# A four-layer decode step and its gradients on one core: where the outer products of the gradients are begun, when the key and value rows are turned, and which queue carries rows of gradients

## The chip, the core and the metric

The kernel runs on one core of a Trainium2 chip. A core has a matrix engine (PE, which also has its own track for weight loads, PEld), a vector engine (DVE), a scalar engine (ACT), GpSimd (POOL) and a sync engine (SP). Each engine takes its instructions strictly in the order in which the program lists them, so an instruction that waits holds up everything behind it on that engine. DMAs are started by SP, ACT or POOL and are then carried out by 16 DMA engines. The metric is the time of one execution on the device in microseconds (us).

## The reference, cut to what matters

One token of width 1024 passes through attention A, MLP B, attention A and MLP B again, with the same weights both times, and then the gradients of all eight inputs are formed for a given output gradient.

```
x = x + A(layernorm(x));  x = x + B(layernorm(x))        # layer 0 of A, layer 0 of B
x = x + A(layernorm(x));  x = x + B(layernorm(x))        # layer 1 of A, layer 1 of B
out, vjp = jax.vjp(f, A_x, A_k_cache, A_v_cache, A_wq, A_wo, B_w1, B_b1, B_w2)
return out, *vjp(grad_out)
```

A has 32 query heads on 4 key-value heads of width 128 and looks at the last 4096 of 32768 cached positions. B is 1024 to 3584 to 1024 with the Mish activation. Everything is bfloat16. The outputs are large: `out_2` and `out_3` (gradients of the key and value caches, 33.5 MB each, zero except for the last 4096 positions of each head), `out_4` and `out_5` (gradients of wq and wo, 8.4 MB each), `out_6` and `out_8` (gradients of w1 and w2, 7.3 MB each), and three vectors. Since there is one token and there are two layers of each kind, the gradient of a weight is a sum of two outer products: a matrix product with only two rows to sum over.

## The kernel before

**Loads.** Weights come in chunks of 1 MB into `ring`, eight slots in SBUF. `Ring.want` queues loads, and `release` (line 77) frees a slot and starts the next queued load on SP's queue (line 68). In the last part of the kernel these are the seven chunks of w2 for the MLP backward of layer 0 (keys "2", 1), the eight chunks of wo for the attention backward of layer 0 (here: wo 0 to wo 7, keys "o", 3), and five chunks of wq (keys "q", 3, t from 0 to 4). Three more wq chunks were kept in the ring, already transposed, from the attention backward of layer 1.

**Zeros.** The zero parts of `out_2` and `out_3` are 56 stores of 1 MB from one zeroed tile. `zeros(n, after)` (line 240) starts n of them on POOL's queue, behind a tiny POOL copy that waits for the value `after`.

**Backward.** A chunk is multiplied by a vector either by DVE (`rowdot`, line 399, one block of 128 x 1024 against a broadcast vector) or by PE: `turned` (line 425) transposes eight 128 x 128 blocks into one of three PSUM buffers `BIG`, copies them back (`evac`, line 278, by DVE or ACT, whichever a running count of planned load says is less busy), and later multiplies them (`mv`, line 439).

The order of the part that the change touches is, in program order:

1. `attn_bwd(1, ...)`, the attention backward of layer 1, whose last loop calls `dn3(t)`.
2. The MLP backward of layer 0: seven chunks of w2, then `dn_b0` (line 810), which multiplies by w1 in SBUF (`W1`) and ends with the backward of the layer norm, `ln_bwd` (line 372). At t = 2 and t = 4 of its loop it starts to collect rows.
3. `attn_bwd(0, ...)`, the attention backward of layer 0: eight chunks of wo ("do"), the products with the values and the probabilities ("dp", hook `dp1`), the products with the keys ("dq", hook `dq1`), eight chunks of wq ("dn", hook `dn1`), and `ln_bwd` again.
4. The tail: `work(10000)` (line 1141) makes everything of the outer products that is left, with PSUM now divided into four `wide` buffers of 128 x 1024.

**Rows of gradients.** The outer products need their vectors as rows. The rows lie in `ROWS`, which is the SBUF of `W1` once w1 has been used; at bases 0, 32, 64 and 96 there are two partitions each (one for each layer). `rowize` (line 953) transposes a vector on PE, copies it to SBUF on ACT (line 959) and starts two small SBUF-to-SBUF DMAs (line 961); `take_back` (line 733) starts one DMA from a small DRAM buffer; `rowize_f` (line 781) does eight small transposes, one ACT copy (line 788) and two DMAs (line 790). All of these DMAs are on ACT's queue. In order there are: GB (2 DMAs), AC, NB, OC, NA (1 each), the two of `rowize_f`, GA (2, in the first step of "do") and DQC (2, in `dq1`).

**DMA lanes.** The DMAs of SP and ACT share eight semaphores in turn. A DMA therefore waits, in its queue, until the eighth DMA before it has landed. By the program's list of waits, and the turn in which the eight are given out, NB waits for wo 0 to have landed, OC for wo 1, NA for wo 2, and the two of `rowize_f` for wo 3 and wo 4.

**Units.** A unit is a product of 128 x 512 (or, with a `wide` buffer, 128 x 1024) of a gradient: one matmul for every 512 columns (line 993 for the four weight gradients; line 1042, two matmuls of 256, for the key and value caches) and one `evac` into a 1 MB staging slot. `store` sends a slot to HBM on SP's queue when it is full (line 971); four of the slots are sent in halves (line 976), once PSUM has been divided anew. No slot is full before the tail, so all stores of units are in the tail. `todo` holds four queues of such generators, and `work(n)` (line 1053) takes n units, going round the four queues. There are 304 units of 512 columns in all. `units_rows(96, ...)` makes `out_8` and reads rows GB and AC; `units_cols(64, ...)` makes `out_6` and reads rows NB and those of `rowize_f`; `units_rows(32, ...)` makes `out_5` from GA and OC; `units_cols(0, ...)` makes `out_4` from NA and DQC. `units_kv` needs the rows of probabilities and of vectors that `kv_rows` (line 1023) turns: 18 transposes and four evacuations for the values, and as many for the keys.

The units before the tail stand in three places: five in `units_b0` (line 802), which `ln_bwd` calls beside the norm of `dn_b0`; five in `dp1`; six in `dq1`.

## Time and profile before

| | us |
|---|---|
| three timed runs | 470.84, 472.27, 469.64; median 470.84 |
| the profiled execution | 475.21 |
| its span between first and last instruction | 473.4 |

| busy in the span | PE | PEld | DVE | ACT | POOL |
|---|---|---|---|---|---|
| us | 352.9 | 276.8 | 263.8 | 229.8 | 38.5 |
| share | 75% | 58% | 56% | 49% | 8% |

The DMA engines moved 183.51 MB in the span, a mean of 388 GB/s; in full stretches the rate is 410 to 425 GB/s. The profiled execution is 4.4 us above the median of the timed runs, so a difference is worked out inside the profile and then taken off the median.

How to read the views: a window line gives, for a stretch of time, the busy us of each engine with the number of instructions in brackets, then the clock that PE was granted (1.00 is full speed), the mean busy share of the 16 DMA engines, and the GB/s that they moved. A timeline line gives start, duration, engine, line of the kernel, operation, destination and source, and in square brackets how long the engine had been idle before it and what released it. `ACTq` and `SPq` are the instruction queues of ACT and SP, where DMAs are started. The chain of waits follows the work that ended last, backwards.

### The profile page before, as it was taken

The page shows a single profiled execution, that of the slowest core. Times are in us where ns is not written, and L with a number is a line of the kernel's source. Part 1 is how long each engine was busy: PE and PEld are TensorE (multiplying, and loading weights), DVE is VectorE, ACT ScalarE, POOL GpSimd, SP SyncE. Part 2 cuts the span into 40 slices and gives each one's busy share as a digit, 9 for nine tenths or more (in the row PEclk, how much of TensorE's full clock was granted, in tenths as well). Part 3 has the DMA queues.
Part 4 walks back from the last instruction along what each step waited for, and adds up shares of the span by engine and source line. Part 5 has one row for each costly group of instructions (what it writes and reads, how often), then busy time and mean ns, then how long its engine had stood idle before and what let it go on. Part 6 is the DMA issues. An engine that isn't in the chain of part 4 may idle for free.

```text
span 473.4 us, 14280 instructions
## 1 busy us (share of the span) xinstructions
PE 352.9 (75%) x6385; PEld 276.8 (58%) x6385; DVE 263.8 (56%) x522; ACT 229.8 (49%) x263; POOL 38.5 (8%) x85
## 2 busy tenths in 40 slices
PE   3746345696688896998797896497897769888880
PEld 3736334596687885898797896387677111111330
DVE  7405820462331259576275876074458678887880
ACT  2402001072146297484176461274154779788880
POOL 4000000000132030101100101002102000000000
PEclk9955555555555588797588555598558555555555
DMA  8999999999999999999999899559998999999997
GB/s 337 422 422 417 419 418 418 422 393 363 395 425 424 419 415 422 414 382 401 424 343 389 309 391 360 225 171 384 424 422 347 412 404 414 420 409 405 412 410 303
DMA packets 28219, 183.51 MB, mean 388 GB/s; under 512 B 3682, under 2 KB 3710, under 8 KB 9342
## 3 DMA queue, kind: packets, MB, share of 16 engines
q1 hardware_dynamic: 19654, 123.78, 65.3%
q0 software_dynamic: 8064, 58.72, 29.9%
q8 instruction: 50, 0.82, 0.7%
q10 hardware_dynamic: 440, 0.10, 0.1%
q14 instruction: 11, 0.09, 0.0%
HBM read 83.94 MB, written 98.62 MB: 386 GB/s over the span
## 4 chain that ended last, share of the span: by engine, by line
PE 50%; DMA 19%; DVE 15%; ACT 6%; issue 5%; ACTq 2%; SPq 0%; DVEq 0%
PE BIG L429 13%; DMA ring<-in_A_wo_dram 8%; PE wide L993 7%; PE BIG L580 4%; PE TP L441 4%; DMA VS<-in_A_v_cache_dram 4%; DVE junk L406 4%; DVE ring L284 4%; DMA W<-in_B_w_dram 4%; PE wide L1042 3%; PE MV L651 3%; ACT ring L287 2%; PE MV L599 2%; DVE VS L284 2%; PE MV L551 2%
## 5 line engine op out<-in xcount | busy, mean ns | idle before, releaser
L287 ACT COPY ring<-BIG 128x1024 bf16<-128x1024 bf16 x73 | 72.2, 1014 | 35.7 <-PE BIG L429 34.1
L429 PE MATMUL BIG<-ident_bf,ring 128*128 128x128 bf16 x872 | 80.8, 254 | 1.9 <-ACT W L287 1.1
L993 PE MATMUL wide<-W 2*128 2x512 bf16 x227 | 68.2, 607 | 11.6 <-ACT W L287 3.0
L429 PEld LDWEIGHTS <-ring 128*128 128x128 bf16 x952 | 70.8, 115 | 4.2 <-issue 3.2
L993 PEld LDWEIGHTS <-W 2*128 2x128 bf16 x240 | 11.8, 101 | 65.3 <-issue 64.6
L406 DVE CUSTOM_DVE_ANT_0 junk<-ring,SC 128x1024 bf16<-128x1024 bf16 x38 | 46.2, 1215 | 2.5 <-PE SC L311 1.1
L441 PEld LDWEIGHTS <-ring 128*128 128x128 bf16 x1024 | 38.5, 100 | 8.4 <-ACT ring L287 4.9
L284 DVE COPY ring<-BIG 128x1024 bf16<-128x1024 bf16 x36 | 24.8, 691 | 31.4 <-PE BIG L429 14.6
L284 DVE CAST ring<-wide 128x1024 bf16<-128x1024 f32 (+1 forms) x29 | 33.2, 1167 | 9.1 <-PE wide L993 5.8
L287 ACT CAST ring<-wide 128x1024 bf16<-128x1024 f32 (+1 forms) x35 | 33.7, 1003 | 7.1 <-PE wide L993 6.0
L287 ACT COPY KT<-BIG 128x1024 bf16<-128x1024 bf16 x22 | 21.6, 1015 | 30.9 <-PE BIG L580 29.3
L287 ACT COPY W<-BIG 128x1024 bf16<-128x1024 bf16 (+1 forms) x24 | 21.4, 1074 | 26.1 <-PE BIG L764 15.8
L248 POOL DMA_DIRECT2D out_dram<-zt x56 | 29.7, 536 | 11.3 <-DMA out_dram<-zt 10.6
L1042 PE MATMUL wide<-W 32*128 32x256 bf16 x122 | 25.7, 403 | 2.5 <-DVE ring L284 1.8
L551 PE MATMUL MV<-OC,ring 128*128 128x1 bf16 x512 | 16.5, 166 | 13.9 <-DMA ring<-in_A_wo_dram 12.8
L551 PEld LDWEIGHTS <-ring 128*128 128x128 bf16 x512 | 15.9, 106 | 14.6 <-DMA ring<-in_A_wo_dram 13.4
L1042 PEld LDWEIGHTS <-W 32*128 32x128 bf16 x128 | 13.4, 121 | 18.2 <-issue 14.4
L471 PE MATMUL MV<-NA,ring 128*128 128x1 bf16 x512 | 15.1, 165 | 10.7 <-DMA ring<-in_A_wq_dram 10.7
L599 PE MATMUL MV<-NB,W 128*128 128x1 bf16 x448 | 16.2, 172 | 9.3 <-DMA W<-in_B_w_dram 6.5
L406 DVE CUSTOM_DVE_ANT_0 junk<-ring,DSX 128x1024 bf16<-128x1024 bf16 x18 | 22.0, 1224 | 0.6
L599 PEld LDWEIGHTS <-W 128*128 128x128 bf16 x448 | 15.9, 118 | 9.8 <-DMA W<-in_B_w_dram 7.2
L471 PEld LDWEIGHTS <-ring 128*128 128x128 bf16 x512 | 14.3, 103 | 11.3 <-DMA ring<-in_A_wq_dram 11.3
(256 smaller groups left out, 552.3 us busy)
## 6 DMA issues: line engine op xcount, KB each, us to landing
out_dram<-zt POOLq DMA_DIRECT2D x56, 1024.0 KB, 14.3
ring<-in_A_wq_dram SPq DMA_DIRECT2D x27, 1024.0 KB
ring<-in_A_wo_dram SPq DMA_DIRECT2D x24, 1024.0 KB
ring<-in_B_w_dram SPq DMA_DIRECT2D x14, 1024.0 KB
W<-in_B_w_dram SPq DMA_DIRECT2D x8, 896.0 KB
out_dram<-ring SPq DMA_DIRECT2D x7, 1024.0 KB
out_dram<-ring SPq DMA_DIRECT2D x12, 512.0 KB
ring<-in_A_k_cache_dram SPq DMA_DIRECT2D x4, 1024.0 KB
```

The costliest lines, as they stand in the source:

```text
L248: nc.gpsimd.dma_start(dst, zt[:])
L284: nc.vector.tensor_copy(dst, src)
L287: nc.scalar.copy(dst, src)
L406: nc.vector.tensor_tensor_reduce(out=out, in0=a, in1=vec, scale=1.0, scalar=acc if i else 0.0, op0=ALU.mult, op1=ALU.add, accum_out=acc)
L429: nc.tensor.transpose(b[:, i * P:(i + 1) * P], block(w, i) if block else w[:, i * P:(i + 1) * P], ident_bf[:])
L441: nc.tensor.matmul(out, lhsT=w[:, i * P:(i + 1) * P], rhs=rhs_of(i), start=fresh[0], stop=last and i == n - 1, skip_group_check=True)
L471: nc.tensor.matmul(q_ps[:, h:h + 1], lhsT=ch[:, h * P:(h + 1) * P], rhs=NA[:, t, l:l + 1], start=(t == 0 and h == 0), stop=(t == TD - 1), ...
L551: nc.tensor.matmul(y_ps[:, dd:dd + 1], lhsT=ch[:, tt, dd * P:(dd + 1) * P], rhs=OC[:, h, l:l + 1], start=(h == 0 and dd == 0), stop=(h == ...
L580: nc.tensor.transpose(b[:, i * P:(i + 1) * P], T[:, g, 8 * b8 + i, :], ident_bf[:])
L599: nc.tensor.matmul(h_ps[:, fb:fb + 1], lhsT=f_block(W1[:, t], fb), rhs=NB[:, t, l:l + 1], start=(t == 0 and fb == 0), stop=(t == TD - 1), ...
L993: nc.tensor.matmul(b[:, 512 * i:512 * i + 512], lhsT=ROWS[base:base + 2, lo:lo + P], rhs=ROWS[base:base + 2, ro + 512 * i:ro + 512 * i + 5 ...
L1042: nc.tensor.matmul(b[:, k * 256:(k + 1) * 256], lhsT=RT[32 * g:32 * g + 32, a, tp, :], rhs=YS[32 * g:32 * g + 32, :], start=True, stop=Tru ...
```

## The change

- `dn_b0` calls `ln_bwd` without work beside its norm. `units_b0` is gone; its two generators (`out_8`, `out_6`) are put into the queues later, ahead of `attn_bwd(0, ...)`.
- `dp1` makes four units in place of five, and no longer calls `kv_rows` nor queues the units of the value cache. `dq1` makes no units, and no longer calls `kv_rows` nor queues those of the key cache.
- `ln_bwd` calls `beside` twice, once before and once after its matmul of the sums. Only `attn_bwd(0, ...)` hands one in: `units_a0`, four units each time. It adds 10 to DVE's planned load, so all eight go to ACT.
- The tail makes 20 units, turns the rows for the value cache and queues its units, makes 20 more, does the same for the key cache, and then makes the rest.
- The twelve DMAs of rows are started by SP in place of ACT, at the same points of the program.
- In `dn3`, one store of zeros waits for t = 5 in place of t = 3.

```
     ln_bwd:
+        if beside is not None:
+            beside()
         nc.tensor.matmul(TP[:, 128:130], lhsT=onesD[:], rhs=st[:], start=True, stop=True)
         if beside is not None:
             beside()
     take_back, rowize_f, rowize:
-        nc.scalar.dma_start(ROWS[...], ...)
+        nc.sync.dma_start(ROWS[...], ...)
-    def units_b0():
-        todo[3].append(units_rows(96, TF, out_8))
-        todo[2].append(units_cols(64, 7, out_6))
-        even()
-        load["D"] += 5
-        work(5)
     dn_b0:
-        return ln_bwd(dnp, sB0["n32"], sB0["rstd"], g, "B0", units_b0)
+        return ln_bwd(dnp, sB0["n32"], sB0["rstd"], g, "B0")
     dn3:
-        if t == 3:
+        if t == 5:
             zeros(1, dnp[:, t:t + 1])
     before attn_bwd(0, ...):
+    todo[3].append(units_rows(96, TF, out_8))
+    todo[2].append(units_cols(64, 7, out_6))
     dp1:
         zeros(4)
         stage_free.extendleft(VS[:, g].rearrange("p t d -> p (t d)") for g in range(G))
-        kv_rows(0, PX, DOC, DOST)
-        for g in range(G):
-            todo[g].append(units_kv(0, g, DOST, out_3))
-        work(5)
+        work(4)
     dq1:
         rowize(DQC, HQ, 0, NOFF)
         zeros(4, DQC[:, 0, 0:1])
-        kv_rows(1, DSX, QC, QST)
-        for g in range(G):
-            todo[g].append(units_kv(1, g, QST, out_2))
-        work(6)
+    def units_a0():
+        even()
+        load["D"] += 10
+        work(4)
     the tail:
     even()
+    work(20)
+    kv_rows(0, PX, DOC, DOST)
+    for g in range(G):
+        todo[g].append(units_kv(0, g, DOST, out_3))
+    work(20)
+    kv_rows(1, DSX, QC, QST)
+    for g in range(G):
+        todo[g].append(units_kv(1, g, QST, out_2))
     work(10000)
```

More of the change, by code (lines that the diff above doesn't have):

```diff
@@ L734, in take_back @@
         r = DR[name][:].rearrange("(n l) p -> l n p", l=2)
-        nc.scalar.dma_start(ROWS[base:base + 2, off:off + r.shape[1] * P].rearrange("l (n p) -> l n p", p=P), r)
+        nc.sync.dma_start(ROWS[base:base + 2, off:off + r.shape[1] * P].rearrange("l (n p) -> l n p", p=P), r)
     x3, st3, sA1 = attn_fwd(1, x2, st2, False, wo_hook1, last_da)
@@ L789, in rowize_f @@
         for l in range(2):
-            nc.scalar.dma_start(ROWS[64 + l:65 + l, NOFF:NOFF + F].rearrange("o (c j) -> o c j", j=512),
-                                rf[:, 512 * l:512 * l + 512])
+            nc.sync.dma_start(ROWS[64 + l:65 + l, NOFF:NOFF + F].rearrange("o (c j) -> o c j", j=512),
+                              rf[:, 512 * l:512 * l + 512])
     def store_f(col):
@@ L823, in dn_b0, with attn_bwd @@
                 rowize_f()
-        return ln_bwd(dnp, sB0["n32"], sB0["rstd"], g, "B0", units_b0)
+        return ln_bwd(dnp, sB0["n32"], sB0["rstd"], g, "B0")
     DENSE = 2
-    def attn_bwd(l, sv, g, wo_key, wq_key, wq_keep, hooks):
+    def attn_bwd(l, sv, g, wo_key, wq_key, wq_keep, hooks, beside=None):
         name = f"A{l}"
@@ L910, in attn_bwd @@
         bigs.remove(SC[1])
-        return ln_bwd(dnp, sv["n32"], sv["rstd"], g, name)
+        return ln_bwd(dnp, sv["n32"], sv["rstd"], g, name, beside)
     turned_q = set()
@@ L960, in rowize @@
         for l in range(2):
-            nc.scalar.dma_start(ROWS[base + l:base + l + 1, off:off + n * P].rearrange("o (t p) -> o t p", p=P),
-                                rt[l:2 * n:2, k, :])
+            nc.sync.dma_start(ROWS[base + l:base + l + 1, off:off + n * P].rearrange("o (t p) -> o t p", p=P),
+                              rt[l:2 * n:2, k, :])
     def store(dst, s, old, new, of, last):
@@ L1128, in dn1 @@
             todo[0].append(units_cols(0, 8, out_4))
-    g0 = attn_bwd(0, sA0, g1, ("o", 3), ("q", 3), (), dict(do=do1, dp=dp1, dq=dq1, dn=dn1))
+    def units_a0():
+        even()
+        load["D"] += 10
+        work(4)
+    g0 = attn_bwd(0, sA0, g1, ("o", 3), ("q", 3), (), dict(do=do1, dp=dp1, dq=dq1, dn=dn1), units_a0)
     g0b = sb([P, TD], BF16, "g0b")
```

## The prediction

> **What bounds the kernel now.** I read the DMA windows first, then the chain of waits in order of time, then the timeline around the place that both point to. Columns of the windows are explained above; these are of the kernel before.

> ```profile
> 270.00:280.00 10.00, 10.00 (x210) 10.00 (x209) 9.56 (x15) 6.19 (x7) 0.00 (x0) 0.50 1.02 386
> ...
> 290.00:300.00 10.00, 3.72 (x89) 3.32 (x86) 4.17 (x20) 1.00 (x1) 1.24 (x3) 0.50 1.01 410
> 300.00:310.00 10.00, 7.25 (x58) 5.30 (x59) 1.91 (x3) 4.71 (x8) 0.00 (x0) 0.58 0.24 98
> 310.00:320.00 10.00, 9.41 (x241) 9.34 (x239) 8.16 (x14) 7.71 (x8) 0.15 (x1) 1.00 0.65 212
> ...
> 370.00:460.00 90.00, 76.74 (x342) 19.57 (x341) 73.25 (x66) 77.22 (x83) 0.00 (x0) 0.50 1.01 412
> 460.00:470.00 10.00, 0.00 (x0) 0.00 (x0) 1.20 (x2) 0.73 (x1) 0.00 (x0) 0.50 1.01 407
> ```

> The DMA engines are full nearly throughout, and in the tail from 370 to 470 without a break, at 407 to 412 GB/s. The last arithmetic is over at about 461, and the DMAs still run 9 us. So the end is set by bytes: it moves by as much as DMA idle time is removed. The one large hole is from 302 to 316. The chain shows what lies in it:

> ```profile
> 289.12 0.76 ACTq L961
> 292.14 2.10 ACTq L735
> 294.28 1.01 ACT W L788
> 295.31 0.75 ACTq L790
> 296.10 5.90 DMA W<-W
> 303.38 1.07 PE BIG L993 x2
> 304.45 0.97 PE SC L311 x8
> ```

> and the timeline what is held up by it:

> ```profile
> 295.47 0.17 DVE L830 CAST GA<-g_B 128x8 bf16<-128x8 f32 x1
> 295.49 1.06 POOL L248 DMA_DIRECT2D out_dram<-zt  x2
> 302.10 0.25 PEld L993 LDWEIGHTS <-W 2*128 2x128 bf16 x4 [7.99 <-issue]
> 302.13 1.01 PE L993 MATMUL BIG<-W 2*128 2x512 bf16 x3 [7.93 <-DMA W<-W]
> ...
> 304.38 1.04 PE L311 MATMUL SC<-ident_bf,GA 128*128 128x128 bf16 x8
> ...
> 312.61 4.41 SPq L68 DMA_DIRECT2D ring<-in_A_wo_dram  x3
> ```

> The five units of `units_b0` need the rows of `rowize_f`. Those rows leave late, because ACT is busy issuing six small DMAs from 289.12 to 294.24 and only then makes its copy (line 788), and the second of their DMAs takes 5.90 us to land. PE stands for 7.93 us with the attention backward of layer 0 behind it, whose input GA is ready at 295.64. Meanwhile the ring is full: five wo chunks and three kept wq chunks. The next load (wo 5) starts only when wo 0 is released, at 312.61, 8.23 us after that attention's first matmul at 304.38. From 302 to 314 the DMA engines have nothing left.

> **The change part by part.**

> *No units at that norm.* The broadcast of GA then follows its cast as in the same code one stage earlier, where the cast at 262.32 is followed by PE at 262.56, 0.24 us later: 295.47 + 0.24 = 295.71 in place of 304.38. Gain 8.67 us on the path. wo 5 follows 8.23 us later, at 303.94. What is late next: the zeros of 295.49 (2 MB) keep the DMAs full until 302 as now, so a hole of about 2 us remains ahead of wo 5, and the slow start from 312.6 to 316 (shares 0.50 and 0.71 in two windows of 2 us) remains too.

> *dp1.* Now the products with DSX start at 338.11, behind 18 transposes and five units; the products with the values end at 333.35. With four units, PE needs three free `BIG` buffers and a fourth that ACT frees at about 334.6 (one ACT evacuation 0.59), so about 335.3. Gain 2.8 us. *dq1.* Now the broadcast ends at 343.02 and the wq transposes start at 348.52; with one small transpose (0.32) between, about 343.4. Gain 5.1 us.

> *Eight units beside the last norm.* PE stands for 1.94 us ahead of line 385 while DVE ends its row products, and the first four units fit there (matmuls of 0.25 to 0.45 us, four ACT evacuations of 0.59). The other four delay the transpose of g0 by about 0.6; the tail, now begun at 368.36, loses that: -0.3 to -1.0, I take -0.5. They need the DQC rows, issued some 15 us earlier, when the last wq load has landed; were these 6 us late, as the slowest row DMA above, that would still be hidden.

> *The path to the tail* so shortens by 8.7 + 2.8 + 5.1 - 0.5 = 16.1 us, to a start at 352.3. *The tail itself* gets longer: 292 of the 304 units in place of 288, at 91.6 us / 288 = 0.32 us each, 1.3 us; and `kv_rows` twice, 36 transposes of 0.107 us (a batch of eight takes 0.85 to 0.88 at half clock), 3.9 us, on a PE that is 85% busy there. Its eight PSUM buffers come from their own counter over the same four `wide` tiles, so each may wait for a unit to be evacuated (1.0 to 1.2 us). Bounds: 0, if all is beside evacuation, and 8 x 2.2 us = 18 us, if every one drains the pipeline. I take 5. Production ends at 352.3 + 91.6 + 6.3 = 450.2, where it was 460.0.

> *The DMAs decide.* From the issue of wo 5 to the last byte at 470.4 there are 157.8 us in which the engines are all but full. The same bytes follow the same issue after the change: eight loads, 14 stores of zeros, all units. Starting at 303.94 they end at 461.7. Two small holes within (358 to 360 at a share of 0.39, 364 to 366 at 0.82: 1.6 us) come when the path waits for `dn1` to issue zeros; with the path 7 us closer to the loads, zeros queue up across them. Hence 460.1 to 461.7. At the tail's start, zeros already issued keep the DMAs full to about 360, so the first stores come in time; production ends 10 us ahead of the last byte, as before. Gain 8.7 to 10.3; I take 9.4.

> *Rows by SP.* Twelve DMAs leave ACT, about 5.1 us of issue on an engine that waits there. SP waits in their place, and behind them in SP's queue stand wo 5 to wo 7 and the wq loads. The rows ahead of wo 5 are ten; the last two need GA, whose transpose comes right after wo 0's (now 308.63, then about 300.0), plus copy 0.25 and two issues of 0.7: done by 302, ahead of the release at 303.94. wo 5 also waits for the lane of AC, wo 6 and 7 for those of NB and OC, all landed by then, as the slowest row now lands at 302.0. Cost 0; were it all serial behind one more 5.9 us landing, wo 5 would start at about 308 and 4 us of the gain would go. First readers of these rows are the units of `dp1` at about 321.

> [...]

> *Zeros at t = 5.* One store moves from 246.26 to about 250.4. The engines were full there but for 0.83 in 248 to 250, and idle at 260 to 264 (0.46, 0.29); the same bytes fill other gaps 40 us ahead of the hole. Bounds: 2.5 us either way of idle time that ends before wo 5 is issued, and no wait of the chain there; 0.

> *PE's clock.* It was granted 0.50 in 270 to 280, though PE was busy for all 10.00 us, and 1.00 after 309, some 4 us into the dense transposes that begin at 304.4. The new start has the same 40 transposes in a row, so I take the same ramp; a later one costs 0.3 us per us. [...]

> Sum: span 473.4 - 9.4 = 464.0; the profiled execution 475.21 - 9.4 = 465.8. The median of the timed runs is 4.4 below that execution: 470.84 - 9.4 = 461.4.

> **The rivals.**

> *Half the gain: SP's queue is held by the rows.* For it: six of the row DMAs wait for lanes of big loads, and an issue took 2.10 us (NA). Against it: wo 5 cannot leave before 303.94 anyway. If wo 5 leaves 4 us late, 465.4.

> *Hardly any gain: the clock stays at 0.50 in the last attention.* For it: a stage of transposes and thin matmuls (one column) stayed at 0.50 for 20 us. There a pair of eight transposes and eight thin matmuls takes 1.07 us; "do" has 26 pairs, 27.8 us in place of the 22.7 from 305.2 to 327.9, and "dn" 17 pairs and 9 single groups of 0.40, 21.8 in place of 15.5. The path loses 11.4 of its 16.1 us, chunks are released every 3.2 us in place of 2.1, and the DMAs wait again: about 2 us at wo 5, 5 us of holes behind. Gain about 2: 468.8. Against it: both attention-like stages before (191 and 235) got 1.00 within 4 to 6 us of dense transposes.

> *Slower: the turned rows choke the tail.* `kv_rows` breaks the rotation of the `wide` buffers. Production ends at 445.2 plus its price; the last stores need about 5 us after production (2 MB at 410 GB/s), so production decides once it ends later than 455, and the kernel is slower than before once it ends later than 465, which takes a price of 20 us, above the 18 of the upper bound; a path that has lost 4 us as well would do. At 18 us and 4 us: 467 + 5 + 3 of span, 475 in the span, 472 as a median. Against it: eight buffers among 150 evacuations.

> **How the numbers follow.** Forecast (8 to 11 us gained) 0.70; half the gain 0.12; hardly any 0.08 (half of it within 0.5%); slower 0.10, with what I have not seen. Runs of this kernel spread by 0.56%, so 0.5% (2.4 us) is about what can be told from no change. Faster 0.70 + 0.12 + 0.04 = 0.86, same 0.04, slower 0.10. The lower end takes the gain to 12.0 (the whole hole and both small ones) and some scatter: 458.0. The upper end takes in half the gain and scatter: 467.0; beyond it lie most of the last two cases and little else, 0.18.

> **What would show it.** Right: no PE wait for `W<-W` ahead of the GA broadcast; wo 5 issued some 8 us earlier; windows of 10 us from 310 on at shares of 0.95 or more; the tail starting near 352; DMAs full to the end, with the last evacuation some 10 us before. Wrong: SP's wo 5 waiting on a `W<-W` DMA; clock 0.50 across "do"; the last evacuation within 5 us of the end, with DMA shares below 0.95 in the tail, which would mean that production and not bytes sets the end.

## The result, and the profile after

The changed kernel takes 466.13 us (median of 16 runs), the kernel before, on the same chip, 471.95 us (16 runs). The ratio is 0.9883, with a 95% interval of 0.9855 to 0.9911: 1.2% faster, a gain of 5.5 us (4.2 to 6.8). The ratio leaves out a run that lies more than 1.5% above the fastest of its kernel (one of each kernel here), so it is not quite the quotient of the two medians. All gains below come from such ratios; the kernel before was run anew beside each set of experiments, with medians of 472.3 to 474.3 us on three chips. The prediction was 461.4 us with a gain of 9.4 us, so the sign was right, the time lies inside the range, and some 40% of the gain is missing. The profiled execution takes 469.29 us, its span is 467.5 us.

The DMA windows of the changed kernel, which answer to those of the kernel before (columns as there: the busy us of PE, PEld, DVE, ACT and POOL, granted clock, DMA share, GB/s):

```profile
290.00:300.00 10.00, 8.03 (x105) 7.46 (x103) 4.33 (x18) 2.17 (x3) 1.23 (x3) 0.56 1.00 409
300.00:310.00 10.00, 9.71 (x250) 9.44 (x247) 7.99 (x14) 8.77 (x9) 0.70 (x2) 1.00 0.72 254
310.00:320.00 10.00, 7.53 (x186) 6.86 (x186) 5.14 (x13) 4.69 (x7) 1.95 (x5) 0.97 1.01 403
...
370.00:380.00 10.00, 8.12 (x30) 1.51 (x30) 7.35 (x7) 8.54 (x10) 0.00 (x0) 0.50 0.82 338
380.00:390.00 10.00, 5.88 (x39) 2.69 (x41) 5.32 (x7) 5.37 (x7) 0.00 (x0) 0.50 0.71 293
390.00:400.00 10.00, 9.40 (x33) 1.22 (x29) 8.38 (x8) 8.28 (x10) 0.00 (x0) 0.50 0.77 316
400.00:410.00 10.00, 8.48 (x33) 1.36 (x31) 7.65 (x7) 8.21 (x11) 0.00 (x0) 0.50 0.95 393
...
450.00:460.00 10.00, 4.30 (x30) 2.41 (x25) 5.05 (x5) 4.43 (x5) 0.00 (x0) 0.50 1.02 404
460.00:470.00 10.00, 0.00 (x0) 0.00 (x0) 0.00 (x0) 0.00 (x0) 0.00 (x0) 0.52 0.47 188
```

The large hole between 300 and 320 has closed but for a share of 0.72 in one window. In its place there are new holes between 370 and 410, in the tail, where the kernel before was full. The timeline of the changed kernel around the stall that was removed:

```profile
293.19 0.16 DVE L824 CAST GA<-g_B 128x8 bf16<-128x8 f32 x1
293.41 1.03 PE L311 MATMUL SC<-ident_bf,GA 128*128 128x128 bf16 x8 [1.49 <-DVE GA L824]
301.72 4.45 SPq L68 DMA_DIRECT2D ring<-in_A_wo_dram  x3
```

PE now multiplies 0.22 us after GA is cast, and SP starts wo 5 at 301.72, where it was 312.61.

To see what became of this, the time is kept as an account. Two executions differ by a few us before the changed place is reached (wo 0 is issued at 275.16 in the profile before and between 269.4 and 274.9 in all later ones, edited there or not), so I count from the issue of wo 0. The rest divides into time in which the DMA engines are busy and idle time (one minus the share, summed over windows of 2 us from 290 to the last byte):

| profile of | from wo 0 to the last byte | DMA idle | difference | idle in 290-330, 330-366, 366-450 |
|---|---|---|---|---|
| before | 195.2 | 14.5 | 180.7 | 11.6, 1.9, 0.9 |
| changed | 191.7 | 11.4 | 180.3 | 2.9, 0.0, 8.4 |

The difference, which stands for the time of the bytes, is 180.5 us either way. The change took away 8.7 us of idle time at the hole and 1.9 at the small holes, 10.6 together, and then gave 7.5 back in the tail. (This account shows 3.5 us of gain for one pair of executions, the timed runs 5.5.)

### The profile page after: what moved, and what is told of

It is laid out like the page before. It is cut to its first block, busy times and chain, and to the rows that moved or that the text cites. A ratio compares the mean times of both kernels' runs of the same rounds, so it can differ in the third digit from the quotient of the medians.

```text
span 467.5 us, 14285 instructions
## 1 busy us (share of the span) xinstructions
PE 354.1 (76%) x6385; PEld 275.5 (59%) x6385; DVE 261.7 (56%) x520; ACT 229.2 (49%) x262; POOL 38.6 (8%) x85
## 5 line engine op out<-in xcount | busy, mean ns | idle before, releaser
L987 PE MATMUL wide<-W 2*128 2x512 bf16 x228 | 64.8, 605 | 11.4 <-ACT ring L287 2.1
L284 DVE CAST ring<-wide 128x1024 bf16<-128x1024 f32 (+1 forms) x28 | 31.8, 1164 | 9.3 <-PE wide L987 7.3
L248 POOL DMA_DIRECT2D out_dram<-zt x56 | 29.6, 534 | 8.5 <-DMA out_dram<-zt 7.8
L287 ACT COPY W<-BIG 128x1024 bf16<-128x1024 bf16 x20 | 18.9, 1161 | 16.0 <-PE BIG L766 16.0
L553 PEld LDWEIGHTS <-ring 128*128 128x128 bf16 x512 | 15.9, 106 | 14.5 <-DMA ring<-in_A_wo_dram 13.4
L473 PEld LDWEIGHTS <-ring 128*128 128x128 bf16 x512 | 14.3, 103 | 11.5 <-DMA ring<-in_A_wq_dram 10.4
L1036 PE MATMUL wide<-W 32*128 32x256 bf16 x128 | 20.9, 403 | 0.1
L287 ACT CAST KT<-wide 128x1024 bf16<-128x1024 f32 x19 | 18.9, 1018 | 2.6 <-PE wide L987 1.8
```

What stands on the lines that cost most here:

```text
L248: nc.gpsimd.dma_start(dst, zt[:])
L284: nc.vector.tensor_copy(dst, src)
L287: nc.scalar.copy(dst, src)
L473: nc.tensor.matmul(q_ps[:, h:h + 1], lhsT=ch[:, h * P:(h + 1) * P], rhs=NA[:, t, l:l + 1], start=(t == 0 and h == 0), stop=(t == TD - 1), ...
L553: nc.tensor.matmul(y_ps[:, dd:dd + 1], lhsT=ch[:, tt, dd * P:(dd + 1) * P], rhs=OC[:, h, l:l + 1], start=(h == 0 and dd == 0), stop=(h == ...
L987: nc.tensor.matmul(b[:, 512 * i:512 * i + 512], lhsT=ROWS[base:base + 2, lo:lo + P], rhs=ROWS[base:base + 2, ro + 512 * i:ro + 512 * i + 5 ...
```

## The experiments

The missing gain is idle time in the tail. The timeline of the changed kernel on PE shows one candidate, the two places at which `kv_rows` turns rows (lines 1020 and 1026; unit matmuls are line 987):

```profile
365.64 0.29 PE L1020 MATMUL wide<-ident_bf,DOC 128*128 128x128 bf16 x1
...
367.09 1.87 PE L1026 MATMUL wide<-ident_bf,PX 128*128 128x128 bf16 x16 [0.29 <-DVE ring L284]
368.89 0.60 PE L987 MATMUL wide<-W 2*128 2x512 bf16 x1
370.06 1.26 PE L987 MATMUL wide<-W 2*128 2x512 bf16 x8 [0.57 <-ACT W L287]
...
382.25 0.62 PE L1020 MATMUL wide<-ident_bf,QC 128*128 128x128 bf16 x2 [1.09 <-ACT ring L287]
383.17 1.86 PE L1026 MATMUL wide<-ident_bf,DSX 128*128 128x128 bf16 x16 [0.29 <-ACT ring L287]
386.13 1.05 PE L987 MATMUL wide<-W 2*128 2x512 bf16 x8 [1.10 <-ACT W L287]
```

Units resume 4.4 us after the first turning began (365.64 to 370.06) and 3.9 us after the second. The other candidate is the grouping of the stores. SP's queue, the changed kernel (each line: start, duration, line, slot; x4 is four stores that leave one behind another):

```profile
395.00 4.24 SPq L965 DMA_DIRECT2D out_dram<-KT  x3
...
406.05 4.66 SPq L965 DMA_DIRECT2D out_dram<-W  x4
415.17 4.28 SPq L965 DMA_DIRECT2D out_dram<-VS  x3
```

and the kernel before, in its tail:

```profile
370.44 0.34 SPq L971 DMA_DIRECT2D out_dram<-W  x1
371.35 1.97 SPq L976 DMA_DIRECT2D out_dram<-VS  x2
373.42 1.20 SPq L971 DMA_DIRECT2D out_dram<-W  x1
375.04 0.87 SPq L976 DMA_DIRECT2D out_dram<-ring  x1
```

`work` goes round the four queues, one piece of work from each in turn, and each queue fills a slot of its own. When all four start together, their slots fill together, and 4 MB become ready every 10 us or so (the groups above start 11.1 and 9.1 us apart). At the 404 to 409 GB/s of the full windows four stores last some 10 us, an estimate, about as long as the production of the next four, so one late group would empty the engines. Before, the first units went to the queues unevenly, slots filled at different times, and stores left in ones and twos. The first theory is thus that the pauses of the turning cost the time, the second that the groups do.

**Undoing parts, one by one.** The kernel before without its five units at the norm, nothing else of the change:

```
     todo[3].append(units_rows(96, TF, out_8)); todo[2].append(units_cols(64, 7, out_6))   # moved ahead of do1_acc
-        return ln_bwd(dnp, sB0["n32"], sB0["rstd"], g, "B0", units_b0)
+        return ln_bwd(dnp, sB0["n32"], sB0["rstd"], g, "B0")
```

> The kernel before with one part of the change: no units beside the norm of the first MLP; the generators of out_8 and out_6 are queued ahead of the last attention; everything else (rows by ACT, rows of keys and values turned in dp1 and dq1, five and six units there) as before. Theory (the stall at that norm is worth its 8.7 us, and the full change loses some of it in the tail): wo 5 is issued about 8.7 us earlier, the tail keeps DMA shares of 0.95 or more in every window of 10 us, and the kernel gains 7 to 10 us, more than the full change with its 5.8. Rival (the gain is lost right behind the norm, whatever is done in the tail): 3 to 6 us.

Measured: ratio 0.9953 (0.9917 to 0.9989), a gain of 2.2 us. The hole went as it should (idle in 290 to 330: 2.9), the small holes before 366 stayed (2.8), and 5.2 us of idle time came in the tail although this kernel turns no rows there. Its windows:

```profile
370.00:380.00 10.00, 8.49 (x36) 1.94 (x33) 7.79 (x7) 8.21 (x11) 0.00 (x0) 0.50 0.80 321
...
390.00:400.00 10.00, 8.48 (x32) 1.27 (x30) 7.60 (x7) 8.21 (x10) 0.00 (x0) 0.50 0.88 365
```

So the expectation fell, and the pauses cannot be the whole cause. On SP's queue its stores leave in fours.

The changed kernel with the rows turned where they were before:

```
     dp1:  zeros(4); stage_free.extendleft(...)
+        kv_rows(0, PX, DOC, DOST); todo[g].append(units_kv(0, g, DOST, out_3)) for each g
         work(4)
     dq1:  zeros(4, DQC[:, 0, 0:1])
+        kv_rows(1, DSX, QC, QST); todo[g].append(units_kv(1, g, QST, out_2)) for each g
     the tail:  the two work(20), kv_rows and appends are gone
```

> The changed kernel, but the rows of the values and keys are turned, and their units queued, in dp1 and dq1 again; no pause for them in the tail. Theory 1 (the two turnings of 4.4 to 5 us in the tail starve the DMAs, which stood idle for 7.7 us between 370 and 408): the idle time in the tail falls below 2 us, the tail starts some 4 to 5 us later than in the changed kernel, and the gain over the kernel before is 9 to 11 us. Theory 2 (the four queues fill their 1 MB slots in step, so stores come late and in bursts, turning or not): idle time in the tail stays at 5 us or more, gain 3 to 6 us.

Measured: 0.9879 (0.9827 to 0.9931), a gain of 5.7 us; idle in the tail 4.0. The profile has half of the tail's idle time gone, at the same start of the tail (81.8 us after wo 0, against 81.6 in the changed kernel). The timed runs do not tell this kernel from the changed one.

The changed kernel with the first 16 slots in halves (line 970) in place of four:

```
-        elif old < h <= new and wide and (last or len(firsts) < 4):
+        elif old < h <= new and wide and (last or len(firsts) < 16):
```

> The changed kernel, but sixteen slots, not four, may be stored in halves, so stores leave earlier. Theory 2 (slots filled in step): DMA idle time in the tail falls from 7.7 to below 3 us, gain over the kernel before 9 to 11 us. Theory 1 (the pauses of the turning): the halves move bytes forward only once, idle time stays at 5 us or more, gain 5 to 7 us.

Measured: 0.9915 (0.9881 to 0.9950), a gain of 4.0 us; idle in the tail 5.3. The idle time is what the first theory expected (5 or more), and the gain is below what either theory did. Its windows:

```profile
370.00:380.00 10.00, 7.43 (x31) 1.52 (x28) 8.04 (x9) 8.22 (x9) 0.00 (x0) 0.50 1.03 418
380.00:390.00 10.00, 7.47 (x40) 2.39 (x38) 6.43 (x6) 6.55 (x7) 0.00 (x0) 0.50 0.97 387
...
400.00:410.00 10.00, 8.48 (x32) 1.36 (x31) 8.12 (x8) 8.16 (x10) 0.00 (x0) 0.50 0.65 263
```

Over the turnings, which stand in the first two of these windows, the engines are as good as full while halves last. The halves run out at 397 on SP's queue, and the window from 400 holds more than half of the idle time. That the pauses empty the engines only where the stores are large is thus suggested by one profile, not shown. Each cure alone moves idle time in the profile and nothing that the timed runs can tell. The kernel before with only the moved store of zeros:

```
-        if t == 3:
+        if t == 5:
             zeros(1, dnp[:, t:t + 1])
```

> The kernel before with one part of the change: the store of zeros in the attention backward of layer 1 waits for t = 5, not t = 3. As forecast: no difference, within 0.5 us of the kernel before. Rival (the 2.3 us by which the changed kernel is ahead at the first matmul of dn_b0, and the DMA idle time at 260 to 264 that is gone there, come from this store): 1.5 to 2.5 us faster.

Measured: 0.9988 (0.9951 to 1.0024), no difference; idle 11.4, 2.0 and 1.0 in the three stretches, as before. Its wo 0 is issued at 269.55, against 275.16 before and 272.24 in the first experiment, which lacks this edit. From the first load of w2 to wo 0 it takes 27.7 us, where the first experiment has 28.9 and the kernel before 32.1. So single profiles leave open whether this part moves wo 0 by some us; the timed runs show nothing of it.

**Both cures together.** The second experiment's kernel, with 24 slots in halves:

```
     (rows turned in dp1 and dq1, as above)
-        elif old < h <= new and wide and (last or len(firsts) < 4):
+        elif old < h <= new and wide and (last or len(firsts) < 24):
```

> The changed kernel with both remedies: rows of values and keys turned in dp1 and dq1 again, and up to 24 slots stored in halves. Theory (the DMAs' idle time in the tail has two sources, the two pauses of the turning and the four queues filling 1 MB slots in step, and the end is the bytes plus the idle time): DMA idle time from 366 to 450 below 2 us, where the changed kernel's profile has 8.4 and the two single remedies 4.0 and 5.4; gain over the kernel before 8.5 to 11 us. Rival (production is too slow whatever the order of stores): idle time stays at 4 us or more, gain 5 to 7 us.

Measured: 0.9787 (0.9728 to 0.9845), a gain of 10.1 us; idle in the tail 1.1. Its windows are full where the changed kernel's are not, and its stores follow one another almost without a gap:

```profile
370.00:380.00 10.00, 9.49 (x34) 1.49 (x33) 8.17 (x8) 9.05 (x11) 0.00 (x0) 0.50 1.03 415
380.00:390.00 10.00, 7.36 (x29) 1.03 (x29) 7.75 (x8) 8.01 (x10) 0.00 (x0) 0.50 1.02 410
390.00:400.00 10.00, 9.20 (x34) 1.41 (x33) 8.14 (x8) 8.80 (x10) 0.00 (x0) 0.50 1.02 412
400.00:410.00 10.00, 7.34 (x30) 1.04 (x29) 7.75 (x8) 8.06 (x9) 0.00 (x0) 0.50 1.02 409
```

```profile
383.81 4.92 SPq L970 DMA_DIRECT2D out_dram<-KT  x4
389.18 4.54 SPq L965 DMA_DIRECT2D out_dram<-KT  x4
393.87 4.81 SPq L970 DMA_DIRECT2D out_dram<-W  x4
```

Stores still leave in fours, but they are halves, and production is a half ahead. The gain is about what the prediction gave the change itself. The interval and that of the changed kernel do not meet (0.9845 and 0.9855). The interval and that of 16 halves with the turning in the tail do not meet; whether that is the place of the turning or the eight further halves was not separated, since 24 halves with the turning in the tail were not run.

The second cure where there is no turning in the tail, that is the first experiment's kernel with halves:

```
     (the kernel before, without units at the norm)
-        elif old < h <= new and wide and (last or len(firsts) < 4):
+        elif old < h <= new and wide and (last or len(firsts) < 24):
```

> The kernel before with no units beside the first MLP's norm, and with up to 24 half stores in place of four. No turning in the tail, rows by ACT. Theory (with no pause in the tail, the four queues filling 1 MB slots in step are all that is in the way): DMA idle time from 366 to 450 falls from the 5.2 us without the halves to below 2 us, gain over the kernel before 5.5 to 8 us in place of 2.2. Rival (something else in the tail eats the gain): gain below 4 us.

Measured: 0.9855 (0.9803 to 0.9908), a gain of 6.9 us, against 2.2 without the halves; idle in the tail 1.5 against 5.2. The two intervals just fail to meet (0.9908 and 0.9917), and the tails start alike (84.8 and 85.4 us after wo 0), so the grouping costs time by itself where five units at the norm no longer put the queues out of step. How much is less sure: 4.7 us by the two ratios, 3.7 by the idle time, and 1.6 by the medians of the two kernels (468.94 and 467.31), which ran on different chips.

**A dose of the turning.** Each `kv_rows` call of the tail made twice (the second writes the same rows again, so this kernel does more work than is needed):

```
+    kv_rows(0, PX, DOC, DOST)
     kv_rows(0, PX, DOC, DOST)
...
+    kv_rows(1, DSX, QC, QST)
     kv_rows(1, DSX, QC, QST)
```

> The changed kernel with each of the two turnings in the tail done twice (the second writes the same values again), which doubles the suspected pause. Theory (the pauses starve the DMAs): production stops for another 4 us each time, DMA idle time in the tail grows from 8.4 to some 14 to 17 us, and nearly all of the gain goes: the kernel is within 2.5 us of the kernel before. Rival (the pauses are beside the point, only the filling of slots in step matters): idle time grows by less than 2 us, gain stays 4 us or more.

Measured: 0.9905 (0.9867 to 0.9943), a gain of 4.5 us; idle in the tail 10.3. The theory expected far more idle time, and the numbers are those of the rival, for which the pauses do not matter. But the timeline shows that the dose was small:

```profile
363.76 0.29 PE L1020 MATMUL wide<-ident_bf,DOC 128*128 128x128 bf16 x1
...
366.87 0.42 PE L1020 MATMUL wide<-ident_bf,DOC 128*128 128x128 bf16 x2
367.08 1.70 PE L1026 MATMUL wide<-ident_bf,PX 128*128 128x128 bf16 x16
368.71 0.39 PE L987 MATMUL wide<-W 2*128 2x512 bf16 x1
369.94 0.62 PE L987 MATMUL wide<-W 2*128 2x512 bf16 x8 [0.84 <-ACT W L287]
```

The pause is 6.2 us in place of 4.4: a second turning costs 1.8 us, close to its own transposes, and the other 2.6 us of the first are paid once; that they are the draining and refilling of the `wide` buffers is argued, not shown. The dose was half of what I had meant, and the idle time rose by 1.9 us; the timed runs do not resolve that, so this experiment decides for neither.

**The remaining parts.** The changed kernel with its rows of gradients on ACT's queue again:

```
-        nc.sync.dma_start(ROWS[...], ...)      (three places)
+        nc.scalar.dma_start(ROWS[...], ...)
```

> The changed kernel with the twelve DMAs of rows started by ACT again, as in the kernel before. As forecast (SP's part is worth nothing): gain within 1.2 us of the changed kernel's 5.8, and wo 5 issued 29 us after wo 0, as there (272.88 to 301.72). Rival (the rows on SP hold up its loads): wo 5 leaves at least 1 us earlier and the gain grows by as much. Rival the other way (ACT's 5 us of issue at that norm were on the path): 2 us or more of the gain go.

Measured: 0.9889 (0.9849 to 0.9929), against 0.9883 for the changed kernel: no difference. In this kernel's profile wo 5 starts 29.7 us after wo 0, and in the first experiment, where ACT also issues the rows, 28.9; in the changed kernel it is 28.8, and up to 29.7 in other kernels with rows by SP.

The changed kernel without its eight units beside the last norm:

```
-    g0 = attn_bwd(0, ..., dict(do=do1, dp=dp1, dq=dq1, dn=dn1), units_a0)
+    g0 = attn_bwd(0, ..., dict(do=do1, dp=dp1, dq=dq1, dn=dn1))
```

> The changed kernel without the eight units beside the last norm; they are made in the tail. The profile has the tail start 2.4 us later relative to that norm than in the kernel before, where the forecast had 0.5; eight units in the tail take about 2.5 us. Theory (a wash): tail starts 2 to 2.5 us earlier and production ends at the same time within 1 us; gain within 1.5 us of the changed kernel's. Forecast's view (units there nearly free): 2 us of the gain go.

Measured: 0.9839 (0.9777 to 0.9902), a gain of 7.6 us; idle in the tail 4.5. The tail starts 76.9 us after wo 0, against 81.6 in the changed kernel. Of these 4.7 us, 2.2 lie behind the row products of the norm (line 383), where the eight units stand; the rest lies ahead of them, where this profile lacks one of the changed kernel's stops of PE, shown below. The time is better by 2 us than the changed kernel's, but the intervals meet, so that it gains is not shown. The same edit on the kernel with both cures:

```
     (rows turned in dp1 and dq1, 24 slots in halves)
-    g0 = attn_bwd(0, ..., units_a0)
+    g0 = attn_bwd(0, ...)
```

> The kernel with both remedies (rows turned early, up to 24 half stores) without the eight units beside the last norm. Theory (the end is the bytes plus the DMAs' idle time; with both remedies there is next to no idle time in the tail left to fill): the tail starts some 4 us earlier after wo 0's issue, but the gain over the kernel before stays that of the kernel with both remedies, 10.1 us (2.13%), within 1.5 us. Rival (PE's path sets the end): 3 us or more faster than that.

Measured: 0.9780 (0.9730 to 0.9829), against 0.9787 with the units: no difference. Its tail starts 81.4 us after wo 0, against 83.3 with the units. Where the tail is full, an earlier start of it is worth nothing that these runs show.

**The rest of the hole.** The kernel with both cures, with one store of zeros moved from `dp1` to the place at which three follow g1:

```
-    zeros(2, g1)
+    zeros(3, g1)
...
-        zeros(4)
+        zeros(3)
```

> The kernel with both remedies, with one store of zeros moved from dp1 to the hook behind g1, where the DMA engines still stand for 3 us ahead of wo 5. Theory (bytes plus idle time): idle time between 290 and 330 falls from 3.0 to below 1.2 us, gain over the kernel before 11 to 13 us. Rival (the zeros delay wo 5 to wo 7 and PE stands for them): gain 9 to 10.5 us.

Measured: 0.9766 (0.9709 to 0.9822), a gain of 11.1 us and 461.74 us, the fastest of all, though not to be told from the kernel with both cures alone. The idle time of 290 to 330 is 0.4 us, and the window in which the changed kernel stood at 0.72 is full in this one:

```profile
300.00:310.00 10.00, 9.16 (x226) 8.81 (x223) 7.40 (x12) 7.70 (x10) 0.71 (x2) 1.00 0.99 354
```

**PE's stops without a cause in the profile.** The changed kernel moved the tail's start less than forecast, and part of that is stops of PE that the profile calls "issue". The timeline of the changed kernel on PE, without a line left out:

```profile
323.03 0.83 PE L857 MATMUL SC<-DOC,VS 128*128 128x8 bf16 x26 [1.74 <-issue]
323.80 0.61 PE L987 MATMUL BIG<-W 2*128 2x512 bf16 x3
325.08 0.58 PE L987 MATMUL BIG<-W 2*128 2x512 bf16 x1 [0.67 <-ACT VS L287]
325.59 2.78 PE L873 MATMUL MV<-DSX,KT 128*128 128x8 bf16 x98
329.23 0.94 PE L873 MATMUL MV<-DSX,KT 128*128 128x8 bf16 x30 [0.86 <-issue]
```

From one stop to the next there are 26 + 3 + 1 + 98 = 128 matmuls, each with its weight load: 256 instructions. If the stops belong to places in the program that lie 256 PE instructions apart, 240 more instructions ahead of them move each by 16, that is by eight matmuls; if they belong to the work done there, they stay where they are. So I added 120 transposes, whose results nobody reads, in the forward pass of the changed kernel (more work than is needed, early and beside loads):

```
     wo_hook0(c):
+        if c < 6:
+            b = big().bitcast(BF16)
+            for i in range(20):
+                nc.tensor.transpose(b[:, (i % 8) * P:(i % 8 + 1) * P], ident_bf[:], ident_bf[:])
```

> The changed kernel with 120 more transposes (240 PE instructions, results not used) in the first attention, where PE waits for loads; every later PE instruction stands 240 places further on. [...] The time of the kernel changes by less than 1.5 us from the changed kernel's in both.

Measured, in the scores of the second attention, which have such a stop in every profile: the changed kernel, and the kernel with the transposes:

```profile
124.86 1.31 PE L490 MATMUL SC<-QC,KT 128*128 128x8 bf16 x44 [2.49 <-issue]
```

```profile
125.07 1.10 PE L490 MATMUL SC<-QC,KT 128*128 128x8 bf16 x36 [1.18 <-issue]
```

The stop moved by eight matmuls, from 44 to 36 before the end of the scores. The stop within the products with the keys moved by eight as well, from 30 to 22 matmuls before their end, and that of 1.94 us beside the last norm is gone. So the stops belong to places in the program.

The time was 0.9809 (0.9768 to 0.9849), a gain of 9.0 us. The expectation was for less than 1.5 us of difference from the changed kernel, and the two intervals do not meet. (The chip was another one; the medians themselves, 464.47 and 466.13, are 1.7 us apart.) Not only the stop of 1.94 us went: in the products with the values, where the changed kernel stops for 1.74 us, this kernel runs through, and the stop of 0.86 us is 0.58. Its tail starts 79.1 us after wo 0, where the changed kernel's starts after 81.6, and has 4.8 us of idle time in place of 8.4, with the groups and the turning as they were. Two more kernels have this tail, or this tail with eight units more: the one with rows on ACT's queue starts it at 82.8 and has 8.6 us of idle time, the one without units beside the norm starts it at 76.9 and has 4.5. So the time at which production begins is a third thing on which the idle time seems to hang, one profile each.

**The account over all.** Idle time, and the rest from wo 0 to the last byte (a profile each), beside the gain in the timed runs:

| kernel | DMA idle | rest | gain of the timed runs |
|---|---|---|---|
| before | 14.5 | 180.7 | |
| changed | 11.4 | 180.3 | 5.5 |
| no units at the norm | 11.0 | 180.9 | 2.2 |
| rows turned early | 6.4 | 180.2 | 5.7 |
| 16 halves | 8.3 | 180.9 | 4.0 |
| zeros at t = 5 alone | 14.4 | 181.8 | 0.6 |
| early and 24 halves | 4.4 | 182.1 | 10.1 |
| turned twice | 12.6 | 181.0 | 4.5 |
| rows by ACT | 12.2 | 180.8 | 5.3 |
| none beside the norm | 8.1 | 180.0 | 7.6 |
| early, 24 halves, none beside | 4.9 | 182.0 | 10.4 |
| early, 24 halves, one zero earlier | 1.7 | 183.5 | 11.1 |
| no units, 24 halves | 6.8 | 182.4 | 6.9 |
| 120 transposes | 7.1 | 181.6 | 9.0 |

The rest is 180.0 to 183.5 in all; the four with 24 halves have the most, 182.0 and above. The idle time saved follows the gain within about 3 us, for single profiles beside medians.

## Why the prediction was right or wrong, point by point

- *The stall at the norm.* Right in mechanism and size. From wo 0, the broadcast of GA starts 8.69 us earlier (29.22 to 20.53; forecast 8.67), wo 5 8.61 us earlier (37.45 to 28.84). The small hole ahead of wo 5 and the slow start remained (2.9 us, the share of 0.72).
- *The small holes before 366.* Filled as forecast: 1.9 us to none, against up to 1.6.
- *`dp1` and `dq1`.* From the products of "do" to the wq transposes it was 19.71 us and is 13.97: 5.7 us gained where 7.9 were forecast. The two stops of PE shown above, 1.74 and 0.86 us, make up the difference; the trace of before has none there, and the prediction has no term for them.
- *Eight units beside the last norm.* Forecast -0.5, measured -2.4 by the stretch from line 383 to the first `wide` matmul (2.67 us before, 5.03 after; 2.79 in the run without them). The first four units would fit PE's wait, but they met a stop of 1.94 us, which the lines of the changed kernel show between the first unit and the next three, with the matmul of the sums (line 387) behind them:

```profile
347.64 0.60 PE L987 MATMUL BIG<-W 2*128 2x512 bf16 x1
350.18 0.61 PE L987 MATMUL BIG<-W 2*128 2x512 bf16 x3 [1.94 <-issue]
350.73 0.59 PE L387 MATMUL TP<-bst,onesD 128*128 128x2 f32 x2
351.44 2.05 PE L987 MATMUL BIG<-W 2*128 2x512 bf16 x4
353.41 0.27 PE L299 MATMUL BIG<-ident_bf,g0b 128*8 128x128 bf16 x1
354.44 1.05 PE L987 MATMUL wide<-W 2*128 2x512 bf16 x7 [0.76 <-ACT W L303]
```

  The stop makes the sums 1.1 us later. The second four units put 2.7 us between the sums and the transpose of g0 (line 299) where it was 1.8, so they cost 0.9, close to the 0.6 of the forecast. The last 0.4 is a longer wait for ACT ahead of the tail.

- *The path to the tail.* The tail starts 11.6 us earlier in place of 16.1 (93.2 to 81.6 us from wo 0; the changed kernel's first `wide` matmul is at 354.44). The three stops account for 3.7 of the 4.5 us that are missing.
- *`kv_rows` in the tail.* Two pauses of 4.4 and 3.9 us; I took 5 for both, with 0 and 18 as bounds. The tail is 8.3 us longer, forecast 6.3.
- *The step that failed: "The DMAs decide".* "The same bytes follow the same issue" holds: 180.3 us against 180.7. What does not hold is that the engines stay "all but full" behind wo 5 and that "the first stores come in time". I carried the fullness of the old tail over to the new one without asking what made it full: without the five units at the norm the stores leave in fours; in the kernel before they left in ones and twos. The new tail has 8.4 us of idle time against 0.9, and the sign of shares of 0.95 or more in every window from 310 on failed (0.71 to 0.82 from 370 to 400). I had tested production by its end alone (455.6, nine us ahead of the last byte at 464.6, close to the forecast of ten), and the idle time lies where production is locally late, from 370 to 408. The runs name three things on which this idle time hangs. The first is groups of four 1 MB stores: halved, with no turning in the tail, they take the gain from 2.2 to 6.9 us. The second is the pauses of the turning: idle time goes from 8.4 to 4.0 when the turning is moved, but with no gain that the timed runs resolve by itself. The third is the late start of the tail: the 120 transposes take the gain to 9.0 with neither cure, and the idle time to 4.8. How much of the missing 3.9 us belongs to each is open, and in the kernel with both cures too; they do not add up, since each takes some 3 to 4 us of the same idle time.
- *Rows by SP.* Worth nothing that the runs show, as forecast: 0.9889 without, 0.9883 with. In the changed kernel's trace no engine waits for one of these rows, so the equal times do not tell how soon they land.
- *Zeros at t = 5.* No effect, as forecast (0.9988).
- *PE's clock.* As forecast: 0.56 in 290 to 300, 1.00 from 300 on, with the transposes dense from 293.4 (0.50 up to 298, 0.79 in 298 to 300, so full speed came some 5 us into them, where the forecast took 4). The rival that it would stay at 0.50 fell. So did that of SP's queue held by the rows.
- *The rival of the choked tail* named the right place with the wrong test. It asked when production would end late, and priced nothing below that point; idle time comes as soon as the stores that are ready run out.

## What to carry to other kernels

Where bytes set the end, price an edit by the DMA idle time that it removes and by the idle time that it can make behind, stretch by stretch: the last evacuation being ahead of the last byte does not show that the stores in between came in time. Ask what makes a full stretch full before counting on it after the change, and whether units that seem idle work also set a phase, as the five units here put four queues out of step. Large stores from several queues served in turn become ready in groups; 24 of them in halves and no interruption in that stretch gave 10 us here, where fewer halves or the interruption's move alone gave nothing beyond the change that the runs resolve. An edit that was expected to change next to nothing in the time, and that moved stops of PE, gave nearly as much (9.0 us); so one good result does not show which cause was cured.

## What the runs showed of the hardware

```profile
q8 instruction: 50, 0.82, 0.7%
```

```profile
q8 instruction: 51, 0.84, 0.7%
```

50 packets with 0.82 MB are about 16 KB each. The changed kernel has 6385 matmuls with as many weight loads, and so 50 places of this kind; with 120 matmuls more there are 51, and the queue moved one packet more. The two counts agree in both kernels. No row shows PE waiting for such a packet, so what PE waits for at these places was not shown.

The pause of a batch of transposes among units was the other surprise: of 4.4 us, the transposes and their copies take 1.8 when repeated. The remaining 2.6 us may be the pipeline of four buffers running empty and filling again, which was not tested apart.
